# Converting two weight tiles per operation, and a flag in place of the zeroing of tiny values

## The chip, the cores and the metric

The kernel runs on one core of a Trainium2 chip. A core has a matrix engine (TensorE, PE in the profile, with its weight loads as PEld), a vector engine (VectorE, DVE), a scalar engine (ScalarE, ACT), a general engine (GpSimd, POOL) and a queue engine (SyncE, SP), which here starts the DMA transfers. The metric is the time on the device of one execution, in microseconds. Three runs of the kernel before took 857.16, 856.85 and 854.94 us, so 856.85 us is the median.

## The reference

A recurrent attention over 4 batches, 8 heads, 768 steps and head dimension 48 feeds two feed-forward layers over the 3072 tokens:

```python
for t in range(S):                       # attention, per batch and head
    cur = einsum('bhd,bhe->bhde', u * kt, vt)
    y[:, :, t] = einsum('bhd,bhde->bhe', rt, state + cur)
    state = wt[..., None] * state + einsum('bhd,bhe->bhde', kt, vt)
x = y.transpose(0, 2, 1, 3).reshape(3072, 384)
h = x @ w_in; x = (h - tanh(h)) @ w_out           # 384 -> 2048 -> 384
h = x @ w_in2; e = exp(h - max(h)); sm = e / (sum(e) + 1e-9)
solu = h * sm                                      # 384 -> 1024
ln = (solu - mean) / sqrt(var + 1e-6) * g_ln
out = ln @ w_out2                                  # 1024 -> 384
```

The four weight matrices come in as 64-bit floats, all else as 32-bit floats.

## The kernel before, in words

**Weights.** The chip computes in 32 bits, so each 64-bit weight is taken apart. A raw tile holds 128 partitions of 384 weights, as pairs of 32-bit words (`L_` the low word, `H_` the high one). `to_f32` (lines 86 to 101) builds the 32-bit value with integer operations: a shift and mask of `H_` on VectorE (line 93), the sign put back on VectorE (line 95), the low word scaled by ScalarE (line 94) and added to the result (line 96, on VectorE or on GpSimd). Two more operations set a weight below 2^-126 to zero: ScalarE squares `H_` as a float (line 92), and VectorE multiplies the value by the comparison of that square with a constant (line 98). `convert` (lines 106 to 111) then splits the value into a rounded part, made by ScalarE (line 110), and the rest, made by a subtraction on GpSimd (line 111). Every matrix product is thus three matmuls: rest times main, main times rest, main times main. There are 16 tiles of each of `w_in` and `w_out` (called conversions A here, 32 tiles) and 8 of each of `w_in2` and `w_out2` (conversions B, 16 tiles).

**Stages.** Attention works in 24 units of 128 tokens (`att_load`, `att_pre`, `att_0` to `att_4`). Four units make a block of 512 tokens, of which there are 6. For each block the first layer runs 16 steps, one for each 128 of its 2048 hidden columns: `part1` makes `hp` by 9 matmuls (line 299) and from it `t`, `y` and `q` on ScalarE and VectorE and `g` on GpSimd; `part2` puts 9 matmuls on `g` into the three accumulators `x2p` (line 318). At the end of a block `x2p` is copied out (`x2o`, line 323). The units of later blocks are computed in between. The tiles A are converted while the first four units and block 0 run, and the tiles B mainly while block 5 runs, since the memory of `w3` and `w4` is taken over from the attention. After block 5 the second layer runs over 24 token tiles (`load_x2`, `b_h` line 379, `norm`, `b_t`, `b_o` line 424).

**Order.** The order in which each engine gets its instructions is set by a scheduler that runs a time model over the whole program. Each engine works through its own instructions strictly in that order. The raw tiles live in a pool of 3 buffers (`cvr`), the values in a pool of 2 (`cv`), and `hp` has 2 buffers as well. `x3` holds the fourth group of head columns of a block. Six DMAs move it to its place in `xs` when the fourth unit of the block is done (line 262).

Of the kernel before, what the change touches and what calls it, by code (L numbers as in the profile page):

```python
# [53 lines left out]
class Kern:
# [7 lines left out]
    def setup(self, const):  # L62
# [6 lines left out]
        self.nflag = 2 * NU + NB * NM  # L69
# [36 lines left out]
    def convert(self, pool, raw, hi, lo, scale=None, add=None):  # L106

        nc = self.nc
        s = self.like(self.to_f32(pool, raw, None, scale, add), hi)
        nc.scalar.copy(hi, s)  # L110
        nc.gpsimd.tensor_tensor(lo, s, hi, ALU.subtract)  # L111


# [163 lines left out]
    def conv_w1(self, pool, raw, m):  # L277
        sl = slice(m * 128, (m + 1) * 128)
        self.convert(pool, raw, self.w1[:, 0, :, sl], self.w1[:, 1, :, sl], add=self.nc.vector)

    def load_w2(self, pool, m):
        raw = pool.tile([128, DM, 2], U32, tag="raw", name="raw2")
# [457 lines left out]
```

## Time and profile before

| what | us |
|---|---|
| median of three runs | 856.85 |
| the profiled execution | 856.38 |
| its span, first to last instruction | 854.7 |
| PE busy in the span | 778.7 |
| DVE busy in the span | 594.1 |
| ACT busy in the span | 473.4 |
| POOL busy in the span | 427.5 |

The span is 1.7 us shorter than the profiled execution. Busy times are unions over the whole span; the kernel has stages with different limits, so a stage is read from its own rows. A row of a group gives the line, the engine, the operation, `out<-in`, the shapes and the count, then the busy time in us and the mean duration in ns, then the idle time before. PEclk is the clock granted to TensorE as a share of full speed.

### The profile page before, as it was taken

The numbers are of one execution on the slowest core, as the hardware profiler recorded it, in microseconds if no ns is written. First come the engines' busy times: TensorE is split into PE (matmuls) and PEld (weight loads), VectorE is DVE, ScalarE is ACT, GpSimd is POOL, SyncE is SP. The second block draws the span as 40 slices with busy tenths as digits, with TensorE's granted clock in tenths as the row PEclk, the third lists the DMA queues.
The fourth block names the chain that finished last, engine by engine and source line by source line (L and its number), as shares of the span: only waits on it lengthen the run. The fifth ranks groups of instructions, "written<-read, shape, count | busy, mean of one in ns | idle before, by whom it ended". The sixth has DMA issues, their size and how long they took to land.

```text
span 854.7 us, 13198 instructions
## 1 busy us (share of the span) xinstructions
PE 778.7 (91%) x4706; PEld 649.1 (76%) x4706; DVE 594.1 (70%) x1058; ACT 473.4 (55%) x936; POOL 427.5 (50%) x410
## 2 busy tenths in 40 slices
PE   4556687799999999999999999987999999999996
PEld 3445465578888888888888888865879999999996
DVE  5999999986665565555555555699467666766763
ACT  4455766756555655565556554676644445444442
POOL 5556689875556555556555554666622111112100
PEclk9766899989999999999999999999999999999999
DMA  9957534524222321142213100332011111111000
GB/s 163 189 123 145 131 92 104 130 47 94 38 38 42 80 45 35 31 87 41 42 32 83 29 20 1 102 120 66 1 55 38 47 38 47 48 38 47 29 28 33
DMA packets 132300, 55.43 MB, mean 65 GB/s; under 512 B 104064, under 2 KB 125696, under 8 KB 132224
## 3 DMA queue, kind: packets, MB, share of 16 engines
q1 hardware_dynamic: 132224, 54.48, 28.2%
q8 instruction: 39, 0.64, 0.3%
q14 instruction: 37, 0.30, 0.1%
HBM read 42.67 MB, written 9.44 MB: 61 GB/s over the span
## 4 chain that ended last, share of the span: by engine, by line
PE 71%; DVE 15%; issue 5%; DMA 3%; POOL 3%; ACT 2%; SPq 1%; DVEq 0%; POOLq 0%; ACTq 0%
PE x2p L318 18%; PE hp L299 18%; PE o L424 12%; PE h L379 11%; PE tp L175 3%; PE qk L211 2%; DVE cv_x L95 2%; PE tt L413 2%; DVE y L308 2%; DVE cv_x L93 2%; PE y L253 2%; PE y L250 2%; DVE cv_s L98 2%; DVE y L305 2%; DMA raw<-in_moe_w_in_dram 1%
## 5 line engine op out<-in xcount | busy, mean ns | idle before, releaser
L299 PE MATMUL hp<-xs,w 128*128 128x512 f32 x864 | 226.4, 402 | 14.0 <-DVE y L305 14.0
L318 PE MATMUL x2p<-g,w 128*128 128x512 f32 x864 | 226.7, 400 | 6.3 <-POOL g L311 4.1
L299 PEld LDWEIGHTS hp<-xs,w 128*128 128x128 f32 x864 | 163.7, 192 | 52.6 <-DVE y L305 17.1
L318 PEld LDWEIGHTS x2p<-g,w 128*128 128x128 f32 x864 | 159.8, 190 | 43.2 <-POOL g L311 6.3
L311 POOL TENSOR_TENSOR g<-y,g 128x512 fp32r<-128x512 f32 x96 | 132.5, 1380 | 6.6
L310 POOL TENSOR_SCALAR g<-y 128x512 fp32r<-128x512 f32 x96 | 69.7, 726 | 129.5 <-DVE y L308 127.6
L305 DVE TENSOR_TENSOR y<-hp,t 128x512 f32<-128x512 f32 x96 | 66.1, 689 | 88.5 <-ACT t L304 73.5
L309 ACT ACTIVATE q<-t,cst 128x512 f32<-128x512 f32 x96 | 69.5, 724 | 83.1 <-DVE y L308 82.9
L424 PE MATMUL o<-w,ts 128*128 128x384 f32 x576 | 110.6, 342 | 2.2 <-DVE st L393 1.1
L379 PE MATMUL h<-w,x2s 128*128 128x512 f32 x432 | 104.0, 392 | 0.7 <-DVE so L399 0.4
L424 PEld LDWEIGHTS o<-w,ts 128*128 128x128 f32 x576 | 100.8, 188 | 4.2 <-DVE st L393 1.3
L379 PEld LDWEIGHTS h<-w,x2s 128*128 128x128 f32 x432 | 80.6, 188 | 17.4 <-PE h L379 0.8
L369 POOL TENSOR_TENSOR x2s<-x2f,x2s 128x384 fp32r<-128x384 f32 x24 | 24.4, 1019 | 130.9 <-issue 102.5
L308 DVE SCALAR_TENSOR_TENSOR y<-q,y 128x512 f32<-128x512 f32 x96 | 85.4, 890 | 5.7 <-ACT q L306 0.4
L304 ACT ACTIVATE t<-hp 128x512 f32<-128x512 f32 x96 | 57.0, 593 | 55.2 <-PE hp L299 54.9
L306 ACT ACTIVATE q<-t,cst 128x512 f32<-128x512 f32 x96 | 69.3, 721 | 2.4
L111 POOL TENSOR_TENSOR w<-cv_s,w 128x384 fp32r<-128x384 f32 x48 | 56.8, 1187 | 25.4 <-ACT w L110 22.3
L211 PE MATMUL qk<-rh,kh 48*128 48x128 f32 x384 | 32.0, 312 | 22.8 <-DVE kh L198 22.8
L175 PE MATMUL tp<-ident,rkw 128*128 128x128 f32 x264 | 42.0, 294 | 11.5 <-DMA rkw<-in_w_dram 5.7
L402 ACT ACTIVATE e<-so 128x1024 f32<-128x1024 f32 x24 | 25.5, 1060 | 47.5 <-DVE so L401 46.4
L211 PEld LDWEIGHTS qk<-rh,kh 48*128 48x128 f32 x384 | 27.0, 212 | 31.1 <-issue 27.5
L392 DVE TENSOR_REDUCE st<-h 128x1 f32<-128x1024 f32 x24 | 29.3, 1223 | 27.6 <-PE h L379 27.6
(112 smaller groups left out, 1196.2 us busy)
## 6 DMA issues: line engine op xcount, KB each, us to landing
raw<-in_moe_w_out_dram SPq DMA_DIRECT2D x16, 384.0 KB, 3.4
rkw<-in_w_dram SPq DMA_DIRECT2D x24, 192.0 KB, 3.8
rkw<-in_r_dram SPq DMA_DIRECT2D x24, 192.0 KB, 4.3
rkw<-in_k_dram SPq DMA_DIRECT2D x24, 192.0 KB, 3.0
vt<-in_v_dram SPq DMA_DIRECT2D x24, 192.0 KB, 3.2
raw<-in_moe_w_in_dram SPq DMA_DIRECT2D x32, 144.0 KB, 3.5
x2d<-x2o SPq DMA_DIRECT2D x18, 256.0 KB, 2.3
x2f<-x2d SPq DMA_DIRECT2D x24, 192.0 KB, 2.5
```

The lines of the kernel that those rows point to most:

```text
L175: self.nc.tensor.transpose(p[:, j], self.rkw[u % 2][:, i, 2 * j:2 * j + 2, :], self.ident)
L211: self.mm(ps[e][:, j], kh[s, j], rh[s, j], start=True, stop=True)
L299: self.mm(hp, self.w1[:, a, j, sl], xs[:, b, j], start=n == 0, stop=n == len(seq) - 1)
L305: v.tensor_tensor(y, hp, t, ALU.mult)
L306: nc.scalar.activation(q, t, AF.Square, bias=self.c_fsb, scale=F_S)
L308: v.scalar_tensor_tensor(y, q, F_E, y, ALU.add, ALU.mult)
L309: nc.scalar.activation(q, t, AF.Relu, bias=self.c_t2, accum_out=self.flags[:, col:col + 1])
L310: g.tensor_scalar(gs[:, 0], y, 1.0, 1.0, ALU.mult, ALU.mult)
L311: g.tensor_tensor(gs[:, 1], y, gs[:, 0], ALU.subtract)
L318: self.mm(self.x2p[d], self.w2[:, a, m, sl], gs[:, b], start=m == 0 and n == 0, stop=m == NM - 1 and n == 2)
L379: self.mm(p[:, f], xs[:, a, j], self.w3[:, b, j, f * 512:(f + 1) * 512], start=q == 0, stop=q == 8)
L424: self.mm(p, ts[:, a, k], self.w4[:, b, k], start=q == 0, stop=q == 3 * NM2 - 1)
```

## The change

Two raw tiles, one of each matrix, are loaded into one buffer of 768 weights and converted together (`conv_a`, `conv_b`). The value pool and the raw pool now hold two buffers of double size. The square and the comparison on VectorE are gone. In their place ScalarE squares `H_` in the raw buffer, and a second operation sums `max(0, constant - square)` into a column of `flags`; a sum above zero sends the whole program to the general path, as the flags for the other fast formulas do already. The addition of the low word is always on VectorE. The weights lie in `wa` (`w1` and `w2` beside each other for each 128 hidden columns) and `wb` (`w3` and `w4`), so that a matmul of `b_h` streams its 512 columns as four pieces of 128. `x3` holds one unit, and its six DMAs follow every unit. `load_x2` lets the DMA write into the second half of `x2s`, where the subtraction then works in place.

```diff
-    def convert(self, pool, raw, hi, lo, scale=None, add=None):
-        nc = self.nc
-        s = self.like(self.to_f32(pool, raw, None, scale, add), hi)
-        nc.scalar.copy(hi, s)
-        nc.gpsimd.tensor_tensor(lo, s, hi, ALU.subtract)
+    def convert(self, pool, raw, hi, lo, col, scale=None):
+        nc, v = self.nc, self.nc.vector
+        flat = raw.rearrange("p i f two -> p (i f) two")
+        H_, L_ = flat[:, :, 1], flat[:, :, 0]
+        x = pool.tile([128, 2 * DM], U32, tag="cv_x", name="cv_x")
+        xf = x.bitcast(F32)
+        nc.scalar.activation(L_, L_, AF.Copy, scale=2.0**-29)
+        v.tensor_scalar(x, H_, 3, 0x3FFFFFF8, ALU.logical_shift_left, ALU.bitwise_and)
+        v.scalar_tensor_tensor(x, H_, 0xC0000000, x, ALU.bitwise_and, ALU.bitwise_or)
+        v.tensor_tensor(x, x, L_, ALU.add)
+        if scale is not None:
+            nc.scalar.activation(xf[:, DM:], xf[:, DM:], AF.Copy, scale=scale)
+        nc.scalar.copy(hi, xf)
+        nc.gpsimd.tensor_tensor(lo, xf, hi, ALU.subtract)
+        Hf = H_.bitcast(F32)
+        nc.scalar.activation(Hf, Hf, AF.Square)
+        nc.scalar.activation(Hf, Hf, AF.Relu, bias=self.c_flag, scale=-1.0, accum_out=self.flags[:, col:col + 1])
...
-        if o == UB - 1:
-            for j in range(KM):
-                for dst, src in ((48, 16 * j), (112, 64 + 16 * j)):
-                    nc.sync.dma_start(out=xs[dst:dst + 16, :, j, :].bitcast(F32), in_=x3[src:src + 16].bitcast(F32))
+        for j in range(KM):
+            for dst, src in ((48, 16 * j), (112, 64 + 16 * j)):
+                nc.sync.dma_start(out=xs[dst:dst + 16, :, j, cols].bitcast(F32), in_=x3[src:src + 16].bitcast(F32))
...
+    def conv_a(self, pool, rpool, m):
+        raw = rpool.tile([128, 2, DM, 2], U32, tag="raw", name="raw_a")
+        self.load_w1(raw[:, 0], m)
+        self.load_w2(raw[:, 1], m)
+        self.convert(pool, raw, self.wa[:, 0, m], self.wa[:, 1, m], 2 * NU + NB * NM + m)
...
+    def conv_b(self, pool, rpool, k):
+        raw = rpool.tile([128, 2, DM, 2], U32, tag="raw", name="raw_b")
+        self.load_w3(raw[:, 0], k)
+        self.load_w4(raw[:, 1], k)
+        self.convert(pool, raw, self.wb[:, 0, k], self.wb[:, 1, k], 2 * NU + NB * NM + NM + k, self.gl[:, k:k + 1])
...
-        x = self.bx.tile([128, KM, 128], F32, tag="x2f", name="x2f")
         s = self.bx.tile([128, 2, KM, 128], F32R, tag="x2s", name="x2s")
+        x = s[:, 1].bitcast(F32)
...
-                    self.mm(p[:, f], xs[:, a, j], self.w3[:, b, j, f * 512:(f + 1) * 512], start=q == 0, stop=q == 8)
+                    self.mm(p[:, f], xs[:, a, j], self.wb[:, b, 4 * f:4 * f + 4, j * 128:(j + 1) * 128], start=q == 0, stop=q == 8)
...
-    cvr = pool(L, "cvr", 3)
+    cvr = pool(L, "cvr", 2)
...
-        if 0 <= s - LAST < NM:
-            K.conv_b(cv, K.load_b(cvr, s - LAST), s - LAST)
+        if 0 <= s - LAST < NM and (s - LAST) % 2 == 0:
+            K.conv_b(cv, cvr, (s - LAST) // 2)
```

The scheduler moves much around this. The first place is VectorE around the first `y` of block 0, the first product with an `hp`. Before, its rows there are these (`cv_x` and `cv_s` are the values of a tile, and the number behind `raw` tells the tile):

```order
L95 SCALAR_TENSOR_TENSOR cv_x_1003<-raw2_1000,cv_x_1003 128x384
L95 SCALAR_TENSOR_TENSOR cv_x_1086<-raw1_1080,cv_x_1086 128x384
L96 ISA cv_x_1003<-raw2_1000,cv_x_1003 128x768
L96 ISA cv_x_1086<-raw1_1080,cv_x_1086 128x768
L98 SCALAR_TENSOR_TENSOR cv_s_1002<-cv_s_1002,cv_x_1003 128x384
L98 SCALAR_TENSOR_TENSOR cv_s_1085<-cv_s_1085,cv_x_1086 128x384
L93 TENSOR_SCALAR cv_x_1098<-raw2_1095 128x384
L95 SCALAR_TENSOR_TENSOR cv_x_1098<-raw2_1095,cv_x_1098 128x384
L96 ISA cv_x_1098<-raw2_1095,cv_x_1098 128x768
L93 TENSOR_SCALAR cv_x_1151<-raw1_1145 128x384
L305 TENSOR_TENSOR y_591<-hp_579,t_589 128x512
```

Nineteen tiles have gone through line 93 by then, 18 through line 95, 15 through line 96 and 17 through line 98. In the changed kernel the same engine has these rows up to its first `y` (now line 316; lines 119 to 121 are the three operations of a pair):

```order
L121 ISA cv_x_931<-raw_a_925,cv_x_931 128x1536
L119 TENSOR_SCALAR cv_x_1020<-raw_a_1014 128x768
L120 SCALAR_TENSOR_TENSOR cv_x_1020<-raw_a_1014,cv_x_1020 128x768
L121 ISA cv_x_1020<-raw_a_1014,cv_x_1020 128x1536
L119 TENSOR_SCALAR cv_x_1073<-raw_a_1067 128x768
L120 SCALAR_TENSOR_TENSOR cv_x_1073<-raw_a_1067,cv_x_1073 128x768
L254 TENSOR_TENSOR st1_135<-ds_653,st0_134 48x4x48 x2
L316 TENSOR_TENSOR y_585<-hp_573,t_583 128x512
```

Nine pairs are complete there and two operations of the tenth are done, so the first `y` stands behind 18 whole tiles and part of two more.

The second place is ScalarE just ahead of the first `t`, from which that `y` is made. Before, it ends with these rows (line 92 squares, 94 scales the low word, 110 rounds, 218 is of the attention):

```order
L92 ACTIVATE cv_s_990<-raw1_985 128x384
L218 COPY kn_133<-kt_613 128x448
L94 ACTIVATE raw2_1000<-raw2_1000 128x384
L92 ACTIVATE cv_s_1002<-raw2_1000 128x384
L110 CAST w1_114<-cv_s_990 128x3x128
L94 ACTIVATE raw1_1080<-raw1_1080 128x384
L94 ACTIVATE raw2_1095<-raw2_1095 128x384
L92 ACTIVATE cv_s_1085<-raw1_1080 128x384
L110 CAST w2_115<-cv_s_1002 128x384
L110 CAST w1_114<-cv_s_1085 128x3x128
L304 ACTIVATE t_589<-hp_579 128x512
```

In the changed kernel the rows there are these (line 118 scales the low word, 127 squares, 128 sums into the flag, 124 rounds):

```order
L118 ACTIVATE raw_a_925<-raw_a_925 128x768
L127 ACTIVATE raw_a_925<-raw_a_925 128x768
L235 COPY kn_133<-kt_607 128x448
L128 ACTIVATE raw_a_925,flags_67<-raw_a_925,cst_66 128x768
L124 CAST wa_115<-cv_x_931 128x768
L118 ACTIVATE raw_a_1014<-raw_a_1014 128x768
L127 ACTIVATE raw_a_1014<-raw_a_1014 128x768
L128 ACTIVATE raw_a_1014,flags_67<-raw_a_1014,cst_66 128x768
L315 ACTIVATE t_583<-hp_573 128x512
```

The square and the flag have been put ahead of the rounding, and the flag of a pair is the last reader of its raw buffer.

The third place is the queue of SP in the attention of block 0. In the changed kernel six DMAs of `x3` stand between the loads of two units:

```order
L161 DMA rkw0_119<-in_w_dram 128x8x48
L278 DMA xs0_139<-x3_138 16x2x128 x6
L161 DMA rkw0_119<-in_r_dram 128x8x48
L161 DMA rkw0_119<-in_k_dram 128x8x48
L162 DMA vt3_124<-in_v_dram 128x8x48
L288 DMA raw_a_925<-in_moe_w_in_dram 48x3x256
```

Before, the queue had one such row in a whole block, with 512 columns in place of 128, behind the fourth unit.

## Rows read from the trace of the kernel before

**Rows 1.** Busy time of each engine in four stretches of the span.
```profile
core 0: us, PE busy (x) PEld busy (x) DVE busy (x) ACT busy (x) POOL busy (x), PEclk, DMA share, GB/s
0.00:91.70 91.70, 49.99 (x400) 40.20 (x400) 77.02 (x151) 47.25 (x103) 53.71 (x58) 0.79 0.80 152
91.70:203.20 111.50, 94.09 (x525) 72.53 (x526) 102.78 (x157) 70.23 (x153) 88.75 (x73) 0.92 0.42 95
541.00:599.00 58.00, 50.11 (x201) 37.79 (x200) 52.76 (x68) 41.80 (x91) 38.23 (x35) 0.97 0.31 98
599.00:627.50 28.50, 28.26 (x124) 22.45 (x122) 12.74 (x18) 16.17 (x32) 16.62 (x17) 1.00 0.00 1
```

**Rows 2.** Timeline of ACT: copies of `x2p` that end blocks 0 and 3.
```profile
203.28 0.59 ACT L323 ACTIVATE x2o<-x2p 128x512 f32<-128x512 f32 x1
...
463.51 1.55 ACT L323 ACTIVATE x2o<-x2p 128x512 f32<-128x512 f32 x3
```

**Rows 3.** Timelines of PE and DVE: the first `hp`, and the first `y` of block 0.
```profile
79.67 5.16 PE L299 MATMUL hp<-xs,w 128*128 128x512 f32 x18
...
92.31 0.68 DVE L305 TENSOR_TENSOR y<-hp,t 128x512 f32<-128x512 f32 x1
```

**Rows 4.** The chain that ended last: nine matmuls back to back.
```profile
309.65 2.05 PE x2p L318 x9
```

**Rows 5.** Groups by line: conversion on DVE and POOL.
```profile
L93 DVE TENSOR_SCALAR cv_x<-raw 128x384 uint32<-128x384 uint32 x32 | 17.6, 550 | 4.9 <-DMA raw<-in_moe_w_in_dram 4.1 <-DMA raw<-in_moe_w_out_dram 0.8
L95 DVE SCALAR_TENSOR_TENSOR cv_x<-raw,cv_x 128x384 uint32<-128x384 uint32 x32 | 27.6, 864 | 0.3
L96 DVE CUSTOM_DVE_ANT_0 cv_x<-raw,cv_x 128x768 uint16<-128x768 uint16 x22 | 16.6, 763 | 0.4
L98 DVE SCALAR_TENSOR_TENSOR cv_s<-cv_s,cv_x 128x384 f32<-128x384 f32 x48 | 40.1, 839 | 4.0 <-ACT cv_s L92 3.7
L111 POOL TENSOR_TENSOR w<-cv_s,w 128x384 fp32r<-128x384 f32 x48 | 56.8, 1187 | 25.4 <-ACT w L110 22.3 <-DVE rh L189 2.8
```

**Rows 6.** By source line: duration in ns, minimum, median and maximum.
```profile
L93 DVE TENSOR_SCALAR cv_x<-raw x32: 328/360/1157, 15.8 to 158.8; 128x384 uint32<-128x384 uint32 x32
L95 DVE SCALAR_TENSOR_TENSOR cv_x<-raw,cv_x x32: 537/548/2319, 16.1 to 159.2; 128x384 uint32<-128x384 uint32 x32
L96 DVE CUSTOM_DVE_ANT_0 cv_x<-raw,cv_x x22: 524/552/1257, 18.4 to 157.7; 128x768 uint16<-128x768 uint16 x22
L308 DVE SCALAR_TENSOR_TENSOR y<-q,y x96: 673/693/1781, 96.6 to 622.5; 128x512 f32<-128x512 f32 x96
```

**Rows 7.** Timelines of DVE and POOL around the longest L95.
```profile
35.88 2.32 DVE L95 SCALAR_TENSOR_TENSOR cv_x<-raw,cv_x 128x384 uint32<-128x384 uint32 x1
...
35.56 1.18 POOL L196 TENSOR_TENSOR inv<-inc,kh 112x512 f32<-112x512 f32 x1
36.69 1.09 POOL L202 TENSOR_SCALAR_AFFINE_SELECT aq<-dg 128x1024 f32<-128x1024 f32 x1
```

**Rows 8.** Groups by line: ACT.
```profile
L92 ACT ACTIVATE cv_s<-raw 128x384 f32<-128x384 f32 x32 | 17.6, 552 | 13.3 <-POOL w L111 6.7 <-DMA raw<-in_moe_w_in_dram 5.3 <-DMA raw<-in_moe_w_out_dram 1.2
L110 ACT CAST w<-cv_s 128x384 fp32r<-128x384 f32 x48 | 24.1, 508 | 22.9 <-DVE cv_s L98 22.8
L402 ACT ACTIVATE e<-so 128x1024 f32<-128x1024 f32 x24 | 25.5, 1060 | 47.5 <-DVE so L401 46.4 <-DVE st L397 1.2
L309 ACT ACTIVATION_READ_ACCUMULATOR q<-t,cst 128x1 f32 x96 | 18.0, 188 | 0.0
```

**Rows 9.** DMA issues: KB each, median us from issue to landing.
```profile
raw<-in_moe_w_out_dram SPq DMA_DIRECT2D x16, 384.0 KB, 3.4
xs<-x SPq DMA_DIRECT2D x36, 64.0 KB, 2.3
x2f<-x2d SPq DMA_DIRECT2D x24, 192.0 KB, 2.5
```

**Rows 10.** Group by line: the matmuls of `b_h` on PE.
```profile
L379 PE MATMUL h<-w,x2s 128*128 128x512 f32 x432 | 104.0, 392 | 0.7 <-DVE so L399 0.4 <-ACT x2o L323 0.2
```

More of the change, by code (lines that the diff above doesn't have):

```diff
@@ L49 @@
 F64_MIN2 = 1.265625 * 2.0**-30
+FLAG_MIN2 = 1.28125 * 2.0**-30
 ACT_SET = "natural_log_exp_and_others"
@@ L68, in setup @@
         self.cst = const.tile([128, 8], F32, name="cst")
[L69 removed]
+        self.nflag = 2 * NU + NB * NM + NM + NM2
         self.flags = const.tile([128, self.nflag], F32, name="flags")
@@ L72, in setup @@
         nc.vector.memset(self.zeros, 0.0)
-        for i, val in enumerate((F_SB, -F_T2, W_LO, -W_HI, -0.5, P_SB, P_MIN)):
+        for i, val in enumerate((F_SB, -F_T2, W_LO, -W_HI, -0.5, P_SB, P_MIN, FLAG_MIN2)):
             nc.vector.memset(self.cst[:, i:i + 1], val)
-        (self.c_fsb, self.c_t2, self.c_lo, self.c_hi, self.c_mhalf, self.c_sb, self.c_min) = (self.cst[:, i:i + 1] for i in range(7))
+        (self.c_fsb, self.c_t2, self.c_lo, self.c_hi, self.c_mhalf, self.c_sb, self.c_min,
+         self.c_flag) = (self.cst[:, i:i + 1] for i in range(8))
     def setup_mask(self, ones):
@@ L127, in att_setup @@
         self.dg = [att.tile([128, 2, 4], F32, name=f"dg{i}") for i in range(2)]
-        self.x3 = xp0.tile([128, 2, BLK], F32R, name="x3")
+        self.x3 = xp0.tile([128, 2, C], F32R, name="x3")
         self.xs = [xp.tile([128, 2, KM, BLK], F32R, name=f"xs{i}") for i, xp in enumerate((xp0, xp1))]
@@ L275, in load_w1, with load_w2 @@
         return raw
[L277 to L282, printed above, removed]
+    def load_w2(self, raw, m):
         self.nc.sync.dma_start(
@@ L423, in b_o @@
             for a, b in ((1, 0), (0, 1), (0, 0)):
-                self.mm(p, ts[:, a, k], self.w4[:, b, k], start=q == 0, stop=q == 3 * NM2 - 1)
+                self.mm(p, ts[:, a, k], self.wb[:, b, k, DM:], start=q == 0, stop=q == 3 * NM2 - 1)
                 q += 1
@@ L473, in fast_path @@
     K.ps_a = pool(R, "ps_a", 3, side="right", space=PSUM)
-    K.w1 = wp.tile([128, 2, KM, FF], F32R, name="w1")
-    K.w2 = wp.tile([128, 2, NM, DM], F32R, name="w2")
+    K.wa = wp.tile([128, 2, NM, 2 * DM], F32R, name="wa")
     K.x2p = [ps_x.tile([128, BLK], F32, name=f"x2p{d}") for d in range(KM)]
@@ L496, in fast_path @@
     first += [(SK * (u - 2) + 1.05, K.att_load, u) for u in range(2, UB + 2)] + [(SK * UB - 1, K.att_pre, UB)]
-    first += [(2.0 * m, lambda m: conv_w(m), m) for m in range(early)]
+    first += [(2.0 * m, lambda m: K.conv_a(cv, cvr, m), m) for m in range(early)]
     for _, f, n in sorted(first, key=lambda e: e[0]):
@@ L515, in fast_path @@
         if 0 <= s < NM - early:
-            conv_w(s + early)
+            K.conv_a(cv, cvr, s + early)
         if s == LAST:
@@ L581, in general_path @@
             for m in range(NM):
-                K.to_f32(rp, K.load_w1(rp, m), w1[:, :, m * 128:(m + 1) * 128])
-                K.to_f32(rp, K.load_w2(rp, m), w2[:, m])
+                for load, out in ((K.load_w1, w1[:, :, m * 128:(m + 1) * 128]), (K.load_w2, w2[:, m])):
+                    K.to_f32(rp, load(rp.tile([128, DM, 2], U32, tag="raw", name="raw"), m), out)
             with (
@@ L600, in general_path @@
             for n in range(NM2):
-                K.to_f32(rp, K.load_b(rp, n), w3[:, :, n * 128:(n + 1) * 128])
-                K.to_f32(rp, K.load_b(rp, n + NM2), w4[:, n], scale=K.gl[:, n:n + 1])
+                for load, out, sc in ((K.load_w3, w3[:, :, n * 128:(n + 1) * 128], None),
+                                      (K.load_w4, w4[:, n], K.gl[:, n:n + 1])):
+                    K.to_f32(rp, load(rp.tile([128, DM, 2], U32, tag="raw", name="raw"), n), out, scale=sc)
             K.bp, K.bs = tp, sp
```

53 lines of the change are left out of this document (17 added, 36 removed).

## The prediction

> **What bounds the kernel now.** I read busy time by stretches first [rows 1]. Up to 91.7 us DVE carries the load: 77.0 us busy, against 47.3 of ACT and 53.7 of POOL. The DMA share of .80 makes 73.4 us of full transfers, so the loads of attention and raw tiles set a floor not far below. From 91.7 to 203.2 us block 0 runs with the rest of conversion A beside it: DVE is 92% busy, PE 84%, POOL 80%, ACT 63%. What PE has to do in a block is seen in the steady part. The copies that end blocks 0 and 3 lie at 203.28 and 463.51 us [rows 2], so three blocks take 260.2 us, 86.7 us each, and the chain there is matmuls back to back [rows 4]. Block 0 lasts 203.3 - 92.3 = 111 us from its first `y`, 24 us over that. Its first `hp` begins at 79.67 us, but the first `y` only at 92.31 [rows 3]: DVE gets to it late, because it works in order and stands in tiles. From 541 to 599 us conversion B does the same to block 5: 201 matmuls at 2.05/9 = .228 us [rows 1, 4] are 45.8 us of work in 58 us, with DVE 52.8 us busy. What follows 599 us is bound by PE. So the gain can come from two stretches: 0 to 203 us and 541 to 599 us.
>
> **DVE's conversion.** Before, a tile takes lines 93, 95, 98 and, in 22 of the 32 tiles A, 96, with means of .550, .864, .839 and .763 us [rows 5]. Two tiles make 2 x 2.253 + 2 x 22/32 x .763 = 5.56 us. The shortest of lines 93, 95 and 96 took .328, .537 and .524 us [rows 6], so the means hold .22, .33 and .24 us an operation of something else. The longest L95, 2.32 us, began at 35.88 and ended at 38.2 us, after two POOL operations that ran from 35.56 to 37.78 [rows 7]. I read the excess as waits on POOL.
>
> After, a pair takes three operations of 768 columns. The slope of such an operation: L308 with 512 columns takes .673 at its shortest, L95 with 384 takes .537 [rows 6], 1.06 ns a column; 768 columns make .537 + .41 = .94. I take .94 for the addition too (doubling .524 gives 1.05), and for line 119 .58, between .53 (same fixed part as L95) and .66 (doubled). With the same excess an operation, .79 in all, a pair costs 2.46 + .79 = 3.25 us and saves 2.3. Over 16 pairs A that is 37 us of DVE, over 8 pairs B (before 2 x 3.02 = 6.03) 22 us.
>
> The same row supports a worse price. L111 on POOL takes 1.187 us for 384 columns [rows 5] and becomes one operation of twice that, so a DVE operation caught behind it waits longer. If the excess doubles with it, a pair costs 2.46 + 1.58 = 4.04 us and saves 1.5, or 24 us over the pairs A.
>
> The Trainium skill, "SBUF — State Buffer", section "Who interferes with whom", says that VectorE and GpSimd share one pair of ports, that it is locked for a whole instruction, and that the loser stands still; a VectorE operation with two inputs in SBUF competes for it. That speaks against the longer POOL operation; the 2.32 us agree with a full stop. By this rule the pair is nearer to 4.04 than to 3.25.
>
> **The first `y`.** Before it, DVE did 19, 18, 15 and 17 of the lines 93, 95, 96 and 98: 10.5 + 15.6 + 11.4 + 14.3 = 51.7 us. After, nine pairs and two operations of a tenth stand there: 9 x 3.25 + 2.07 = 31.3. DVE alone would bring it from 92.3 to 71.9 us (79.6 with the double excess). The transfers have their floor at 73.4 us, and the first four units have a chain of their own through PE, ACT and POOL, whose length the rows don't give. No gain at all leaves 92.3. I take the middle, 82.1 us.
>
> **Block 0.** DVE's 102.8 us lose about 27 (the other 6 to 7 pairs A at 2.3, and early tiles B at 3 each two), and leave some 76. ACT: per pair before 2 x (.552 + .552 + .508) = 3.22 us (line 94 taken as 92). Its slope is (1.060 - .508)/640 = .86 ns a column [rows 8]; at 768 the scale, the square, the flag and the rounding take .88, .88, .97 + .19 for reading the sum (as L309's .188) and .84, together 3.76, .5 more. With the preparation of pairs B ACT comes from 70.2 to some 79 us. POOL loses about half of its additions of the low word and stays near 80. PE with 86.7 us is then the largest in the block. Its work filled 86.7/111 = .78 of this stretch (it was 94.1 us busy, at a granted clock of .92, between its levels of 1.2 and 2.4 GHz [rows 1]) and fills 1.00 of the steady one. While conversion still interleaves I take .90, about halfway: 96.3 us. x2o comes at 82.1 + 96.3 = 178.4 us in place of 203.3: 24.9 us earlier.
>
> **Conversion B.** 45.8 us of matmuls filled .79 of this stretch; at the same .90 they take 50.9 us in place of 58: 7.1 us.
>
> **Edits that I cost at nothing.** The six `x3` DMAs follow every unit, 144 in place of 36; one lands in 2.3 us [rows 9], so even one behind another the 24 of a block fill 55 of 86.7 us. A unit's data are wanted only when its whole block is there; uncovered, the last unit's six delay block 0 alone, as they did before. The work of the units themselves covers the rest. The raw load of a pair has to wait for the flag, last of ACT's operations on it: two landings of 3.4 us one behind the other [rows 9], 3.8 us of ACT and 3.3 of DVE make a turnaround of at most 14 us without waits. Two buffers give a pair in 7 us; from 15.8 us, the first L93 [rows 6], that is nine pairs by 79 us. `load_x2` in place waits for the matmuls of the tile two before; 2.5 us of landing [rows 9] and two operations stand against a token tile's (854.7 - 627.5)/24 = 9.5 us, so it is covered. `w3` read as four pieces of 128 columns: 432 matmuls of .392 us [rows 10]. No row shows such pieces; I take 0, the nearest row being L379 itself. One fixed .07 us more for each would cost 30 us, all of it on PE's path.
>
> **The sum.** Against the profiled execution: 24.9 + 7.1 = 32 us. The span of 854.7 becomes 822.7, the execution 824.4. The median of the runs is .5 us above the profiled one, so 825 us; from here times stand on that scale.
>
> **Rivals.**
> First, PE at once: first `y` at 73.4 us, share 1.00 in both stages. Then x2o at 160.1 and B in 45.8: 43.2 + 12.2 us less, 801 us. For it: DVE's load falls below PE's. Against it: POOL at 80% keeps feeding `g`, and in-order queues never interleave perfectly.
>
> Second, another engine takes over: ACT, in order, with single operations of .9 us ahead of every `t`, or the double excess on DVE. With the first `y` at 88 and a share of .84, x2o comes at 88 + 103.2 = 191.2 and B takes 54.5: 12.1 + 3.5, 841 us. With no gain in the first `y` at all, 850 us. For it: every ACT row grows and DVE's mean is far above its minimum. Against it: ACT has 41 us idle in block 0.
>
> By the rule of the ports above, with DVE at 4.04 us a pair, the first `y` would be at 86, midway between 79.6 and 92.3, and the sum near 829 us. That is inside the forecast's own range.
>
> Third, on the other side: the raw buffers. Before, three buffers let tile n+3 load while three are in work. After, there are two pair buffers, each held until ACT has done the flag, which stands behind whatever ACT waits for. If a turnaround becomes 25 us, a pair takes 12.5, and the sixteenth comes at 16 + 15 x 12.5 = 203.5 us; block 0 needs it for its last step, ends some 15 us later (its conversion and two steps of 86.7/16 = 5.4 us), and the kernel is 15 us slower, 872 us. It decides from about 23 us a turnaround. For it: DVE sat idle 4.1 + .8 us for raw tiles [rows 5], and ACT waited for them too [rows 8]. Against it: my working gives 14 us.
>
> Fourth, the strided reading of `w3` costs more than .07 us a matmul: as four separate matmuls of 128 columns, with a fixed part each, it would be over 30 us, and the kernel not faster (855 to 880 us). And the flag could fire, taking the general path, milliseconds; weights drawn from a normal distribution have none that small.
>
> **Chances.** The forecast, with its own range of 812 to 835 us: .70. PE at once: .08. Another engine: .12. Raw buffers: .05. Strided reading: .04. The flag: .01. What this kernel's measurement can tell from no change is .3%, 2.6 us. Faster takes the first three but for .02: .88. Same: .04, from the ends of the second and fourth. Slower: .08. The range goes from 803 to 846 us: below to the first rival, above through most of the second.
>
> **What would show it.** In the profile after: the first `y` at 75 to 88 us; x2o of block 0 at 170 to 187; DVE's busy share in block 0 under 85% and PE's at .9; line 119 at .53 to .66 and lines 120 and 121 at .94 to 1.05 at their shortest; the longest of them beside POOL's 768-column subtraction; the stretch of conversion B at 51 us; the matmuls of `b_h` still at .39 us; the second layer still 227 us. The steady blocks at 86.7 us. I am wrong if DVE or ACT idles on raw loads between 20 and 180 us, if the matmuls of `b_h` are longer, or if PE's busy share in block 0 stays at .84.

## The result, and the profile after

Four runs of the changed kernel took 843.12 to 845.29 us, median 844.0, against 856.2 for the kernel before: ratio 0.986, interval 0.984 to 0.988. It is 12 us faster where 32 were forecast. The profiled executions, 843.12 and 856.38 us, differ by 13.3.

Where the 13.3 us lie is read from the copies of `x2p` that end the blocks, ScalarE's timeline of the changed kernel (start us, us, engine, line, operation):

```profile
193.68 0.60 ACT L334 ACTIVATE x2o<-x2p 128x512 f32<-128x512 f32 x1
...
452.74 1.55 ACT L334 ACTIVATE x2o<-x2p 128x512 f32<-128x512 f32 x3
...
612.24 1.59 ACT L334 ACTIVATE x2o<-x2p 128x512 f32<-128x512 f32 x3 [2.49 <-PE x2p L329]
```

and of the kernel before, for the end of block 5 (blocks 0 and 3 are [rows 2]):

```profile
626.56 1.59 ACT L323 ACTIVATE x2o<-x2p 128x512 f32<-128x512 f32 x3 [2.50 <-PE x2p L318]
```

Block 0 ends 9.6 us earlier and block 3 10.8. From block 3 to block 5 it is 159.5 in place of 163.05 us, 3.5 less. From there to the span's end it is 841.3 - 612.24 = 229.1 in place of 228.1 us, 1 more. Sum: 10.8 + 3.5 - 1.0 = 13.3.

Busy time by stretches, as in [rows 1], with block 0 and conversion B where they lie now:

```profile
core 0: us, PE busy (x) PEld busy (x) DVE busy (x) ACT busy (x) POOL busy (x), PEclk, DMA share, GB/s
0.00:91.70 91.70, 50.15 (x406) 40.18 (x406) 63.11 (x113) 52.38 (x94) 44.74 (x46) 0.83 0.83 155
91.70:193.70 102.00, 90.98 (x524) 71.39 (x525) 87.97 (x118) 78.71 (x153) 77.52 (x58) 0.95 0.49 113
531.50:585.00 53.50, 48.32 (x197) 37.07 (x196) 39.27 (x38) 43.11 (x81) 40.77 (x29) 0.97 0.23 78
```

VectorE has lost 13.9 us up to 91.7 and 14.8 more in block 0, now 86% busy there. TensorE's matmuls in block 0's stretch are about as many as before (524 for 525) and took 90.98 us in place of 94.09, at a granted clock of .95 in place of .92: 3.1 us of what block 0 gained go with the higher clock, the rest is less waiting. VectorE's conversion rows in the first 195 us (the columns of [rows 5]; lines 119 to 121 stand for 93, 95, 96 and 98), and L319, the old L308:

```profile
L319 DVE SCALAR_TENSOR_TENSOR y<-q,y 128x512 f32<-128x512 f32 x18 | 20.2, 1120 | 2.9 <-ACT q L317 2.6
L121 DVE CUSTOM_DVE_ANT_0 cv_x<-raw_a,cv_x 128x1536 uint16<-128x1536 uint16 x16 | 19.5, 1221 | 1.2 <-ACT t L315 0.5
L120 DVE SCALAR_TENSOR_TENSOR cv_x<-raw_a,cv_x 128x768 uint32<-128x768 uint32 x16 | 18.3, 1144 | 0.3
L119 DVE TENSOR_SCALAR cv_x<-raw_a 128x768 uint32<-128x768 uint32 x16 | 11.4, 710 | 19.6 <-DMA raw_a<-in_moe_w_out_dram 8.0 <-DMA xs<-x 6.3 <-DMA raw_a<-in_moe_w_in_dram 5.2
```

The last row shows what is late now. A pair costs .710 + 1.144 + 1.221 = 3.08 us, but ahead of line 119 VectorE sat idle 19.6 us, nearly all for DMAs, where the old L93 sat 4.9 [rows 5]. The timeline around the first `y` shows the same:

```profile
79.31 5.35 PE L310 MATMUL hp<-xs,wa 128*128 128x512 f32 x18
...
87.69 0.56 DVE L119 TENSOR_SCALAR cv_x<-raw_a 128x768 uint32<-128x768 uint32 x1 [5.23 <-DMA raw_a<-in_moe_w_in_dram]
...
91.24 0.59 ACT L315 ACTIVATE t<-hp 128x512 f32<-128x512 f32 x1
...
92.49 0.69 DVE L316 TENSOR_TENSOR y<-hp,t 128x512 f32<-128x512 f32 x1
```

The first `hp` begins at 79.31 us where it began at 79.67 [rows 3], and the first `y` has not moved either: 92.49 for 92.31. The `hp` of that `y` is done by about 82 us (an estimate: half of the 5.35 us of its row, which holds two). But ScalarE and VectorE wait in order for the ninth raw pair, and `t` and `y` stand behind it. On ScalarE (the first row is the end of the seventh pair's flag, which frees the buffer that the ninth pair needs):

```profile
71.01 0.19 ACT L128 ACTIVATION_READ_ACCUMULATOR raw_a<-raw_a,cst 128x1 f32 x1
...
87.65 0.90 ACT L118 ACTIVATE raw_a<-raw_a 128x768 uint32<-128x768 uint32 x1 [4.32 <-DMA raw_a<-in_moe_w_in_dram]
```

and in SyncE's queue:

```profile
28.67 1.73 SPq L293 DMA_DIRECT2D raw_a<-in_moe_w_out_dram  x1
30.51 4.87 SPq L278 DMA_DIRECT2D xs<-x  x6
...
41.52 3.79 SPq L278 DMA_DIRECT2D xs<-x  x6
...
76.02 3.77 SPq L278 DMA_DIRECT2D xs<-x  x6
79.84 0.58 SPq L288 DMA_DIRECT2D raw_a<-in_moe_w_in_dram  x1
```

The ninth pair's buffer is free at 71.2 us, but its loads are issued from 79.84 on: the eighth pair's loads and then the six `x3` DMAs of the fourth unit stand in front of them, and these wait for that unit's data until 76.02. The data are there at 87.65. Such a set of six takes the queue 3.8 to 4.9 us, and it now comes after every unit.

### The profile page after: what moved, and what is told of

It reads as the page before. It is cut to its first block, busy times and chain, and to the rows that moved or that the text cites. A ratio compares the mean times of both kernels' runs of the same rounds, so it can differ in the third digit from the quotient of the medians.

```text
span 841.3 us, 13250 instructions
## 1 busy us (share of the span) xinstructions
PE 773.4 (92%) x4706; PEld 646.9 (77%) x4706; DVE 550.4 (65%) x949; ACT 486.0 (58%) x912; POOL 406.4 (48%) x376
## 4 chain that ended last, share of the span: by engine, by line
PE 77%; DVE 7%; DMA 5%; issue 3%; SPq 3%; ACT 3%; POOL 2%; DVEq 0%; ACTq 0%; POOLq 0%
PE x2p L329 20%; PE hp L310 20%; PE o L431 12%; PE h L386 11%; PE tp L192 3%; PE qk L228 3%; PE tt L420 2%; DMA raw_a<-in_moe_w_out_dram 2%; PE y L270 2%; PE y L267 2%; DVE cv_x L119 1%; SPq L161 1%; PE kt L234 1%; DVE cv_x L120 1%; DVE y L319 1%
## 5 line engine op out<-in xcount | busy, mean ns | idle before, releaser
L329 PE MATMUL x2p<-g,wa 128*128 128x512 f32 x864 | 223.8, 399 | 10.9 <-POOL g L322 9.5
L310 PE MATMUL hp<-xs,wa 128*128 128x512 f32 x864 | 226.1, 402 | 4.4 <-DVE y L316 4.4
L329 PEld LDWEIGHTS x2p<-g,wa 128*128 128x128 f32 x864 | 159.7, 189 | 48.0 <-POOL g L322 12.7
L310 PEld LDWEIGHTS hp<-xs,wa 128*128 128x128 f32 x864 | 163.4, 192 | 42.4 <-DVE y L316 7.1
L320 ACT ACTIVATE q<-t,cst 128x512 f32<-128x512 f32 x96 | 69.6, 725 | 78.6 <-DVE y L319 78.4
L431 PE MATMUL o<-wb,ts 128*128 128x384 f32 x576 | 110.1, 341 | 2.1 <-DVE st L400 1.1
L386 PE MATMUL h<-wb,x2s 128*128 128x512 f32 x432 | 103.9, 392 | 1.6 <-DVE so L406 1.4
L431 PEld LDWEIGHTS o<-wb,ts 128*128 128x128 f32 x576 | 100.4, 188 | 4.3 <-DVE st L400 1.3
L386 PEld LDWEIGHTS h<-wb,x2s 128*128 128x128 f32 x432 | 80.6, 188 | 18.5 <-issue 1.8
L319 DVE SCALAR_TENSOR_TENSOR y<-q,y 128x512 f32<-128x512 f32 x96 | 87.8, 915 | 9.7 <-ACT q L317 4.4
L192 PEld LDWEIGHTS tp<-ident,rkw 128*128 128x128 f32 x264 | 31.5, 147 | 21.8 <-issue 17.7
L402 DVE TENSOR_REDUCE part<-e 128x32 f32<-128x1024 f32 x24 | 29.3, 1220 | 28.4 <-ACT e L401 28.4
```

Source lines behind the costliest of these rows:

```text
L192: self.nc.tensor.transpose(p[:, j], self.rkw[u % 2][:, i, 2 * j:2 * j + 2, :], self.ident)
L310: self.mm(hp, self.wa[:, a, m, j * 128:(j + 1) * 128], xs[:, b, j], start=n == 0, stop=n == len(seq) - 1)
L319: v.scalar_tensor_tensor(y, q, F_E, y, ALU.add, ALU.mult)
L320: nc.scalar.activation(q, t, AF.Relu, bias=self.c_t2, accum_out=self.flags[:, col:col + 1])
L329: self.mm(self.x2p[d], self.wa[:, a, m, sl], gs[:, b], start=m == 0 and n == 0, stop=m == NM - 1 and n == 2)
L386: self.mm(p[:, f], xs[:, a, j], self.wb[:, b, 4 * f:4 * f + 4, j * 128:(j + 1) * 128], start=q == 0, stop=q == 8)
```

## The experiments

Sixteen kernels were run, each against the kernel before on the same chip. After the profiles, the question was no longer what VectorE saves but what the savings run into. All times below are medians; a time stands beside 844.0 for the changed kernel, and a ratio beside its .986 (.984 to .988).

**First: loads, buffers and the flag.** `x3block` puts the `x3` DMAs back to the block's end:

```diff
-        for j in range(KM):
-            for dst, src in ((48, 16 * j), (112, 64 + 16 * j)):
-                nc.sync.dma_start(out=xs[dst:dst + 16, :, j, cols].bitcast(F32), in_=x3[src:src + 16].bitcast(F32))
+        if o == UB - 1:
+            for j in range(KM):
+                for dst, src in ((48, 16 * j), (112, 64 + 16 * j)):
+                    nc.sync.dma_start(out=xs[dst:dst + 16, :, j, :].bitcast(F32), in_=x3[src:src + 16].bitcast(F32))
```

> The changed kernel with x3 as before: 512 columns, six DMAs after the fourth unit of a block. To make room, the low part of the last pair of w1/w2 is not kept (its matmuls read the high part in its place), same instructions. Theory S (the issue queue of SP is the limit between 15 and 80 us: its x3 DMAs take 3.8 to 4.9 us after each of the first three units, with raw loads and attention loads behind them): first hp at 72 to 76 us in place of 79.3, first y at 84 to 88 in place of 92.5, time 834 to 840 us against 844. Theory R (two raw buffers, held until the flag, are the limit): first y within 1 us, time 843 to 845.

Measured: 841.2 us, ratio .9821 (.9802 to .984), 3 us better than the changed kernel. First `hp` at 76.4, first `y` at 89.5, block 0 ends at 189.07 us, 4.6 earlier. Every number moves the way that S says and none reaches its range: S holds in kind, at less than its size, and its interval meets the changed kernel's at .984.

`raw3` has a third raw buffer, `both` that and `x3block`:

```diff
-    cvr = pool(L, "cvr", 2)
+    cvr = pool(L, "cvr", 3)
```

> The changed kernel with three raw pair buffers in place of two. To make room, the low parts of the last two pairs are not kept (their matmuls read the high parts), same instructions. Theory R (raw buffers are the limit): DVE's idle time for raw loads, 12.8 us between 16 and 92 us, falls under 4, first y at 83 to 87 in place of 92.5, x2o of block 0 at 184 to 188 in place of 193.7, time 833 to 838 us. Theory S (SP's issue queue): the loads are issued no earlier, first y within 2 us, time 842 to 845.

> Three raw pair buffers and x3 as before, the low parts of the last three pairs not kept. If R and S both hold and add up: first y at 75 to 80 us, time 825 to 832. If one alone holds: the time of the better of the two single runs.

Measured: 856.3 us (1.0003; .9988 to 1.0018) and 854.4 us (.9972; .9958 to .9987). Both theories fail here. In `raw3` the idle time did go: VectorE waits 3.8 us for raw loads from 16 to 92 us in place of 12.8, and is busy 39.46 of 44 us from 16 to 60 us (changed kernel: 32.67). But the first `hp` comes later (minimum, median and maximum in ns, then first and last start in us):

```profile
L313 PE MATMUL hp<-xs,wa x36: 388/396/776, 83.7 to 99.0; 128*128 128x512 f32 x36
```

and in the waits of 16 to 92 us (who waits, for whom, us in total, times, longest) PE waits for VectorE's `kh`, a step of the attention:

```profile
PE qk L228 <- DVE kh L215: 18.8, 4, 8.6
```

By itself that row proves little: the changed kernel has 16.3 us there, and `x3block`, which is faster, 18.1. The order on VectorE says more. The last step of the fourth unit, whose result the first `hp` needs, stands at these times, in the changed kernel and in `raw3`:

```profile
75.21 0.55 DVE L274 TENSOR_TENSOR xs<-x2p,xs 112x384 fp32r<-112x384 f32 x1
...
77.72 0.56 DVE L274 TENSOR_TENSOR xs<-x2p,xs 112x384 fp32r<-112x384 f32 x1
```

Before it VectorE has begun 7 pairs in the changed kernel, 8 in `raw3` and 9 in `both`, where it comes at 79.5 us. An earlier load let conversion go ahead of the attention, and the first `hp` waits for the attention. The wait for raw pairs was real, but without it the kernel is slower. That order is only a part of the loss, though: the first `y` of `raw3` is 1.2 us later (93.7), the rest of block 0 takes 6.7 us more, of which 5.0 go with a lower granted clock (95.98 us busy at .91 in place of 90.98 at .95, for 520 and 524 matmuls), and the second layer 3.2 us more. Why the second layer takes longer there no run shows.

`noflag` leaves out the two operations of the flag:

```diff
-        Hf = H_.bitcast(F32)
-        nc.scalar.activation(Hf, Hf, AF.Square)
-        nc.scalar.activation(Hf, Hf, AF.Relu, bias=self.c_flag, scale=-1.0, accum_out=self.flags[:, col:col + 1])
```

> The changed kernel without the flag's two ScalarE operations on a pair (the check of tiny weights is left out). Theory R: a raw buffer is free about 2 us earlier in a turnaround, first y 4 to 8 us earlier, time 836 to 840. Theory A (ScalarE in order is the limit, 2.1 us more a pair ahead of t): the same at the first y, and also PE's share in block 0 up to .90 or more, time 832 to 838. Theory S: first y within 2 us, 841 to 844.

Measured: 840.2 us, .9806 (.9785 to .9827). VectorE begins its ninth pair at 81.81 us in place of 87.69, and the first `y` comes at 85.9 us, 6.6 earlier, as R and A expected. Block 0 ends at 190.42, only 3.3 earlier: 104.5 us from the first `y`, a share of .83, so A's second half fails. The whole flag costs 4 us in pairs.

**Second: floors, and the change's two halves.** `nocompute` replaces the conversion of a pair:

```diff
-        nc.scalar.activation(L_, L_, AF.Copy, scale=2.0**-29)
-        v.tensor_scalar(x, H_, 3, 0x3FFFFFF8, ALU.logical_shift_left, ALU.bitwise_and)
...
+        nc.scalar.activation(hi, H_.bitcast(F32), AF.Copy, scale=1.0e-6)
+        nc.gpsimd.tensor_tensor(lo, hi.bitcast(F32), hi.bitcast(F32), ALU.subtract)
```

> The changed kernel with all loads, but a pair is converted by one ScalarE copy of 768 and one GpSimd subtraction of 768 (the integer operations on VectorE, the scaling and the flag are left out, the weights are not the reference's, and the general path is never taken). Theory L (the transfers, DMA share 0.96 from 16 to 60 us, set the attention of the first four units and so the first hp): first hp at 74 to 80 us as now (79.3). Theory E (conversion on DVE and ACT delays the attention): first hp at 60 to 68 us. For block 0 both expect a share of PE above .95: from the first y to x2o at most 92 us in place of 101.2.

Measured: 821.6 us (.9604; .9584 to .9623).

```profile
L299 PE MATMUL hp<-xs,wa x51: 387/396/773, 74.0 to 99.9; 128*128 128x512 f32 x51
L305 DVE TENSOR_TENSOR y<-hp,t x6: 676/692/692, 83.2 to 106.2; 128x512 f32<-128x512 f32 x6
```

With nothing of the conversion left on VectorE the first `hp` comes at 74.0 us, in L's range, and the first `y` at 83.2 us. Block 0 ends at 174.54, 91.3 us from there, a share of .95. It is not a strict floor: its last part takes 231.1 us, where `flagonly` below has 226.1, and `flag_raw2` below has its first `hp` at 71.5 us with all of the conversion. So the transfers alone do not hold the first `hp` at 74.

`noload` loads raw tiles for the first two pairs only:

```diff
-        raw = rpool.tile([128, 2, DM, 2], U32, tag="raw", name="raw_a")
-        self.load_w1(raw[:, 0], m)
-        self.load_w2(raw[:, 1], m)
+        raw = self.raws[m % 2]
+        if m < 2:
+            self.load_w1(raw[:, 0], m)
+            self.load_w2(raw[:, 1], m)
```

> The changed kernel with all conversion operations, but raw tiles loaded for the first two pairs alone; the two buffers are converted again for each further pair, in the same order of operations (weights are not the reference's, and the general path is never taken). Theory L: without 22 pairs' transfers and issues the first hp comes at 60 to 70 us, and DVE does not idle before line 119. Theory E: first hp at 76 to 80 us.

The loads of the eight pairs B were kept in this run, so 14 pairs' loads are left out, not the 22 that the expectation names. Measured: 846.5 us (.9895; .9875 to .9915) by two runs, 2.5 us above the changed kernel, but the intervals touch. Leaving out the loads gained nothing. First `hp` at 85.5 us, later than either theory allows, and in the waits of 16 to 90 us:

```profile
PE qk L228 <- DVE kh L215: 21.6, 3, 10.1
```

It is `raw3` again, and further: VectorE has begun 10 pairs before the last step of the fourth unit, which comes at 81.9 us. Over the changed kernel, `raw3`, `both` and `noload` these are 7, 8, 9 and 10 pairs, with that step at 75.2, 77.7, 79.5 and 81.9 us. On single tiles a third buffer moves the first `hp` the same way, from 71.5 us (`flag_raw2`) to 75.7 (`flagonly`). L fails; E's mechanism agrees with these rows, but its 76 to 80 us do not.

`zeropair` keeps the pairs and the zeroing:

```diff
+        nc.scalar.activation(lo, H_.bitcast(F32), AF.Square)
...
+        v.scalar_tensor_tensor(xf, lo.bitcast(F32), F64_MIN2, xf, ALU.is_ge, ALU.mult)
...
-        nc.scalar.activation(Hf, Hf, AF.Square)
-        nc.scalar.activation(Hf, Hf, AF.Relu, bias=self.c_flag, scale=-1.0, accum_out=self.flags[:, col:col + 1])
```

> The changed kernel with pairs, but with the zeroing of before in place of the flag: ScalarE squares 768 columns and VectorE multiplies by the comparison (the square stands in the place of the low part until that is written). A pair has one VectorE operation more (1.1 to 1.3 us) and one ScalarE operation less (1.2 us), and the raw buffer is free without the flag. Theory P (pairing alone brings the gain): 840 to 847 us. Theory F (leaving out the zeroing brings it): 850 to 856 us.

`flagonly` puts the flag into the kernel before and leaves the rest of that as it was (the operations of `to_f32` but for the square and the comparison now stand in `convert` itself):

```diff
-        s = self.like(self.to_f32(pool, raw, None, scale, add), hi)
...
+        s = self.like(xf, hi)
...
+        nc.scalar.activation(Hf, Hf, AF.Square)
+        nc.scalar.activation(Hf, Hf, AF.Relu, bias=self.c_flag, scale=-1.0, accum_out=self.flags[:, col:col + 1])
```

> The kernel before with the flag in place of the zeroing, on single tiles of 384 columns and three raw buffers; weights, x3 and the second layer as before. VectorE loses 48 x .84 = 40 us, ScalarE gains 48 x .7 = 34 us. Theory F: 840 to 848 us. Theory P: 851 to 857 us. If ScalarE in order is what costs: above 857.

Measured: `zeropair` 858.5 us (1.0038; 1.0024 to 1.0052) and `flagonly` 834.6 us (.9752; .9736 to .9768). Both lie on F's side, and beyond its ranges. The flag alone brings 20.6 us; the pairs with what they need alone cost 3, and on top of the flag they take 9.4 away. `flagonly` by blocks:

```profile
194.90 1.08 ACT L338 ACTIVATE x2o<-x2p 128x512 f32<-128x512 f32 x2
...
452.79 1.55 ACT L338 ACTIVATE x2o<-x2p 128x512 f32<-128x512 f32 x3
...
607.37 1.59 ACT L338 ACTIVATE x2o<-x2p 128x512 f32<-128x512 f32 x3 [3.86 <-PE x2p L333]
```

Block 3 ends where the changed kernel's does (452.79, 452.74). The difference is in blocks 4 and 5, 154.6 us in place of 159.5 (`nocompute` has 154.7 there, no less), and in the rest, 833.5 - 607.37 = 226.1 us in place of 229.1: 7.9 us together, as far as the two profiled executions are apart.

**Third: is it the length of the operations?** `splitall` cuts every operation of the changed kernel in two, by a loop over the two halves around the whole conversion, `splitpool` only GpSimd's:

```diff
-        nc.gpsimd.tensor_tensor(lo, xf, hi, ALU.subtract)
+        for h in (slice(0, DM), slice(DM, 2 * DM)):
+            nc.gpsimd.tensor_tensor(lo[:, h], xf[:, h], hi[:, h], ALU.subtract)
```

> The changed kernel with its pair buffers, x3 by unit and all additions on VectorE, but every conversion operation in two of 384 columns. Theory W (operations of 768 columns, 0.9 us on ScalarE and 1.9 on GpSimd, stand longer in front of the attention and of t and y in queues that work in order): 833 to 839 us. Theory B (two pair buffers, x3 by unit, the layout cost it): 842 to 850 us.

> The changed kernel with GpSimd's subtraction alone in two of 384 columns. Theory K (GpSimd's 1.9 us operation keeps VectorE's operations with two inputs waiting: L319 in block 0 at 1.145 us against .972 before): L319 there at or below 1.0 us and 836 to 841 us. Theories W and B: 842 to 845 us.

Measured: 849.9 us (.9914; .9885 to .9943) and 843.2 us (.9837; .9807 to .9866). Shorter operations are worse or the same, so W falls; `splitall` also does twice as many operations, at .54 us each where one of double width takes .94 at its shortest. Of K one row agrees: with the halves L319 (here L320) takes less in the first 195 us,

```profile
L320 DVE SCALAR_TENSOR_TENSOR y<-q,y 128x512 f32<-128x512 f32 x18 | 18.3, 1020 | 0.3
```

1.02 for 1.12 us. But the pair's own operation with two inputs takes more, 1.285 us for 1.144 (here too L120):

```profile
L120 DVE SCALAR_TENSOR_TENSOR cv_x<-raw_a,cv_x 128x768 uint32<-128x768 uint32 x16 | 20.6, 1285 | 0.3
```

So the halves did not shorten VectorE's work as a whole, and the time stays within the intervals: the length of GpSimd's operation is not what costs the 9.4 us.

`flag_dve` and `flag_lo` start from `flagonly`. The first moves the additions, the second the place of the flag's values:

```diff
-        add = self.nc.vector if 3 <= m < 9 else None
+        add = self.nc.vector
```

```diff
-        nc.scalar.activation(Hf, Hf, AF.Square)
-        nc.scalar.activation(Hf, Hf, AF.Relu, bias=self.c_flag, scale=-1.0, accum_out=self.flags[:, col:col + 1])
...
+        nc.scalar.activation(lo, self.like(H_.bitcast(F32), lo), AF.Square)
+        nc.scalar.activation(lo, lo.bitcast(F32), AF.Relu, bias=self.c_flag, scale=-1.0, accum_out=self.flags[:, col:col + 1])
```

> The kernel with the flag on single tiles (834.6 us) with all additions of the low word on VectorE, as the changed kernel has them. If this is part of what the changed kernel loses: 837 to 842 us (10 x .76 = 7.6 us more on VectorE). If VectorE has room since the zeroing went, and GpSimd's 10 x 1.13 us were in the way: 829 to 834 us.

> The kernel with the flag on single tiles (834.6 us), the square and the flag's sum made in the place of the low part, so that the raw buffer is free after one ScalarE read and need not wait for VectorE. Theory R (the raw buffer held until the flag costs): 829 to 833 us. Otherwise: 834 to 836 us, or above, since GpSimd's subtraction now waits for the flag.

Measured: 836.0 us (.9756; .9729 to .9783) and 836.9 us (.9769; .9742 to .9796). Where the additions run makes no difference. In `flag_lo` block 0 ends at 189.43, 5.5 earlier than in `flagonly`, but blocks 4 and 5 take 159.3 us, 4.7 more.

**Fourth: the parts that pairing brought along,** one at a time in `flagonly`. `flag_x3unit` has the six `x3` DMAs after every unit, by the change's own lines (the reverse of `x3block`). `flag_x2in` loads in place, and `flag_raw2` has two raw buffers:

```diff
-        x = self.bx.tile([128, KM, 128], F32, tag="x2f", name="x2f")
         s = self.bx.tile([128, 2, KM, 128], F32R, tag="x2s", name="x2s")
+        x = s[:, 1].bitcast(F32)
```

```diff
-    cvr = pool(L, "cvr", 3)
+    cvr = pool(L, "cvr", 2)
```

`flagA_lo` has the two lines of `flag_lo` for the tiles A alone.

> The kernel with the flag on single tiles (834.6 us) with x3 by unit, as the changed kernel has it. Theory S (SP's issue queue: six x3 DMAs hold it 3.8 to 4.9 us after each unit): first y 3 to 6 us later than 88.1 and 837 to 841 us. If x3 by unit costs nothing on single tiles: 833.5 to 836 us.

> The kernel with the flag on single tiles with the in-place load of x2s. If the wait of the load for the matmuls of two tiles before is what the second layer lost (227.5 us after the last x2o in place of 224.5): 837 to 838 us, with the second layer at 227. If not: 834 to 835.5 us and 224.5.

> The kernel with the flag on single tiles with two raw buffers in place of three. Theory B (with two buffers there is no load waiting ahead, and block 5 or the start pays): 838 to 846 us, blocks 4 and 5 together at 157 us or more in place of 154.6. If the number of buffers does nothing: 834 to 836 us.

> The kernel with the flag on single tiles, with the square and the sum in the place of the low part for the tiles A alone. From flag_lo the end of block 0 at 189.4 us in place of 194.9, and from the flag on single tiles blocks 4 and 5 at 154.6 us in place of 159.3: 829 to 832 us. If the scheduler's order undoes one of the two: 834 to 838 us.

Measured: `flag_x3unit` 839.1 us (.9804; .9786 to .9823), `flag_x2in` 837.8 (.9795; .9776 to .9815), `flag_raw2` 838.0 (.9788; .9767 to .9809), `flagA_lo` 833.5 (.9734; .9712 to .9756). Against `flagonly` by ratios the first three cost 4.5, 3.7 and 3.1 us, 11 together, where the changed kernel has lost 9.4; the interval of `flag_raw2` touches that of `flagonly`, those of the other two do not. By stages of the profiles the three add up as well: to 5.6 us more in blocks 4 and 5, where the changed kernel has lost 4.9, and to 3.6 in the rest, where it has lost 2.9 (at the end of block 3, where it has lost nothing, they come to 1.0 less). Where each pays is less clean. With `x3` by unit the first `y` is 1.8 us later (S wanted 3 to 6), block 0 ends at 195.3 us as before, and blocks 4 and 5 take 157.8 us, 3.2 more. With `x2s` in place the last part takes 833.6 - 605.7 = 227.9 us, 1.8 more, half of what the median lost. With two raw buffers the first `y` comes at 83.2 us, 5 earlier, and yet block 0 ends at 196.3, 1.4 later. `flagA_lo` ends block 0 at 191.07 and takes 154.7 us for blocks 4 and 5; it beats both kernels, but its interval does not part it from `flagonly`.

## Why the prediction was wrong

**VectorE's savings in a pair: right.** A pair was put at 3.25 us and took 3.08 with waits; minima of .54, .94 and .94 us were forecast as .58, .94 and .94. By the means of their rows the pairs A take 49.2 us of VectorE where about 87 were spent, 38 less for 37 forecast. The double excess did not come, though the means still hold .17, .20 and .28 us over the minima. ScalarE's 768-column operations took .91, .92, 1.01 + .19 and .83, as forecast. What became free on VectorE was less than that, though: the forecast had 20.4 us up to the first `y` and about 27 in block 0, the stretches show 13.9 and 14.8. Some 7 us went back to slower neighbours up to the end of block 0. L308 (now L319) rose from .972 to 1.145 us in the mean of 17, and the addition to the attention's state (before L238, now L255) by two thirds:

```profile
L238 DVE TENSOR_TENSOR st<-st,inc 48x192 f32<-48x192 f32 x10 | 6.4, 641 | 0.2
...
L255 DVE TENSOR_TENSOR st<-st,inc 48x192 f32<-48x192 f32 x10 | 10.7, 1068 | 0.2
```

**The step that failed first: "DVE alone would bring it from 92.3 to 71.9 us", and the middle of that and 92.3.** It gave 10.2 us; measured, none. Two things were wrong in it. A `y` needs its `hp`, and [rows 3] already had the first `hp` at 79.67 us; half of the 5.16 us there for its nine matmuls and .6 for `t` make 82.9. My lower end lay 11 us before its own input. No run has a first `y` before 83.2 us: `nocompute` has it there with no conversion at all on VectorE, and `flag_raw2` with all of it and its first `hp` at 71.5. I noted that the first four units had a chain "whose length the rows don't give", and then gave it no weight.

But 82.9 would still have left me nearly all of the 10.2 us. What held the `y` until 92.49 is the ninth pair, behind which it stands with the first operations of the tenth. I had "nine pairs by 79 us", from a turnaround of 14 us without waits. VectorE began the ninth at 87.69 us: two buffers, a flag as their last reader and a queue that waits at the `x3` DMAs made it 8.7 us a pair ((87.69 - 17.71)/8, from the first L119) and not 7. `noflag` has the ninth pair at 81.81 and the first `y` 6.6 us earlier; `x3block` has the ninth at 78.95 and the first `y`, there behind ten whole pairs, 3 us earlier. So the saved work of VectorE turned into waiting for loads. My own sign for being wrong, VectorE or ScalarE idle on raw loads between 20 and 180 us, is what the profile shows.

**The second: block 0 at a share of .90.** It took 101.2 us from the first `y`, a share of .86, so 9.8 us came in place of 14.7. The form of the term was wrong too. I treated the first `y` and the share as independent. In the runs they trade: `flag_raw2` has the first `y` 5 us earlier than `flagonly` and ends block 0 later, `noflag` gains 6.6 us at the first `y` and 3.3 at the end, and the changed kernel ends block 0 before `flagonly` with its first `y` 4.4 us later. Conversions that do not stand before the first `y` stand behind it. The end of block 0 is one quantity. `nocompute`, without the conversion's work, has it at 174.5 us; my 178.4 left 4 us for the whole of that work.

**The third: conversion B.** 7.1 us forecast, 3.5 measured. `flagonly` shows that VectorE's saving was enough for 8.5 there (154.6 for 163.05); what pairing brought took 5 of it back. The second layer, put at no change, took 1.0 us more; the blocks 1 to 3 between gave 1.2 that I had not foreseen.

**Edits costed at nothing.** `x3` by unit is not free: 3 us in the changed kernel, 4.5 on single tiles. I had priced the 24 DMAs of a block by their landing, 55 of 86.7 us, where there is room, and not their place in a queue in the first 80 us, where three more sets of 3.8 to 4.9 us, and the waits for their data, stand between loads that are wanted. The in-place `x2s` costs up to 3.7 us against my "it is covered". The strided reading of `wb` by `b_h` did cost nothing: L386 has a mean of .392 us, as L379 had [rows 10].

**The rivals.** PE at once is refuted. The raw buffers' rival described a real wait, 12.8 us of VectorE from 16 to 92 us, but `raw3` shows that taking it away gains nothing. That another engine takes over was nearest in size (841 us), but no engine does: in block 0 VectorE is 86%, ScalarE 77% and GpSimd 76% busy. Its variant without any gain in the first `y` was put at 850; by its own terms (x2o at 92.3 + 103.2 = 195.5, 7.8 + 3.5 us less) it is 845.5, and those are nearly the numbers that came, for another reason. What holds, as I read it, is order: engines that work in order, each with conversion and attention mixed, wait for one another. That is read from the rows (the ninth pair ahead of `t` and `y`, the pairs ahead of the fourth unit's last step) and agrees with `raw3` and `noload`; a run that changes the order alone was not made, so it is not shown.

**The page's rule.** The Trainium skill, "SBUF — State Buffer", "Who interferes with whom", says that a VectorE instruction with two inputs in SBUF contends with a GpSimd instruction that reads SBUF, and that the one that comes second waits until the first is done. L319, which has two such inputs, agrees in kind: 1.12 us in the mean, .676 at its shortest. By that rule alone I would have gone to 829 us, with a pair at 4.04; it took 3.08. And `splitpool`, with GpSimd's operation halved, has L319 at 1.02 but L120 at 1.285; it is worth 2 us by the ratios, which is within their intervals.

What stays open: why `x3` by unit costs blocks 4 and 5 in `flag_x3unit` and the start in `x3block`, and how the pairs' loss of blocks 4 and 5 comes about. Every edit also changes the scheduler's order everywhere, and a run holds both.

## What to carry to other kernels

Before a saving on a busy engine is turned into time, look for the input of the thing it delays: a result cannot come earlier than its own operands, so the row of the operand bounds the gain as long as the operand itself does not move. Then follow the queue that feeds the engine: work that is saved there can turn into waiting for loads. A run with the work left out (here 821.6 us) tells about how much there is to win; a forecast near it is too good. When a change has a part that saves work and a part that rearranges it, run them apart: here the flag on single tiles takes 834.6 us, 9 better than both together. And a wait that is removed may only let other work go first, as in `raw3`.

## What the runs showed of the hardware

SyncE's issue of one `x3` DMA took .59 us at the median, with 128 columns (144 of them in the changed kernel, .591) as with 512 (36 in the kernel before, .592): the number of DMAs counts there, not their size. Some were longer, six together up to 4.87 us. A DMA that waits for its data holds the queue: the ninth pair's loads, with their buffer free at 71.2 us, were issued from 79.84. GpSimd's subtraction of 768 columns took 1.84 us at the median, of 384 columns 1.12 (the kernel before) or 1.01 (`splitpool`), so doubling its width saved 9 to 18%; VectorE's operation with two inputs (L95, now L120) took .942 at its shortest for 2 x .537, which saves 12%. In block 0 TensorE's busy time went with the granted clock, for 520 to 525 matmuls: 90.98 us at .95 (changed kernel), 94.09 at .92 (before), 95.98 at .91 (`raw3`). The pairs did save engine time, and the kernel got no time from it.
